# Gating two groups of tokens at a time in a gated-attention and top-2 expert kernel

## The chip, the cores and the metric

One core of a Trainium2 chip runs the whole kernel. The metric is the device time of one execution in microseconds (us). The engines meant below are TensorE (PE, its weight loads PEld), VectorE (DVE), ScalarE (ACT), GpSimd (POOL) and SyncE (SP). SP and POOL issue the transfers: SP the plain ones, POOL the indirect ones, whose rows go to or come from addresses that the kernel has computed. Each engine runs its own queue strictly in order, so an instruction that waits holds up everything behind it on that engine.

## The reference

The first half is a gated linear attention with a complex decay, the second a top-2 mixture of 8 experts on its output.

```python
# q, k, v, a_re, a_im: (4, 8, 768, 48), B=4 batches, H=8 heads
mag = np.sqrt(a_re * a_re + a_im * a_im)
scale = np.minimum(mag, 0.999) / (mag + 1e-06)
for t in range(S):
    S = (a * scale)[t] * S + k[t] v[t]^T          # complex state, 48 x 48 per head
    y[t] = q[t] @ S.real
x = y.transpose(0, 2, 1, 3).reshape(3072, 384)
noisy = x @ w_gate + log1p(exp(x @ w_noise)) * noise       # (3072, 8)
top2, weights = two largest of noisy, softmax over the two
out[t] = sum over the two experts e of weight * (relu(x[t] @ w1[e]) @ w2[e])   # 384 -> 1024 -> 384
```

(The recurrence and the last lines are abridged here.)

## The kernel before

**Attention.** The 3072 tokens are 24 tiles of 128: six groups g = 0 to 5 (blocks of the sequence), with B = 4 tiles in each (one per batch). Tile n is tile n % 4 of group n // 4. For each tile PE transposes q and k (`tr_unit`, L293), multiplies them (`sc_unit`, L302), DVE masks the product (L303), and `y_unit` (L349 and L351) multiplies by v and by the state, after which ACT copies the result out of PSUM into `xT` (L352, remembered as `YC[n]`). `x_unit` turns that tile into rows of tokens and ACT writes them into `xr` (L360), the buffer from which rows are sent on. A buffer `xr` holds the four tiles of one group, 400 numbers of each token.

**Gating.** When the tiles of a group are done, `gate_logits` (L363 to 376) multiplies them by the gate weights, turns the result and leaves 16 logits of each token in `lz`. `gate_dispatch` (L386 to 421) then runs a chain of some 28 short DVE instructions with three ACT exponentials among them (`gates` and `softplus`, L36 to 74): noisy logits, the two best experts of each token (L57 and L59, one instruction for each tile), their weights, which go straight into `xr` (L73). A few small matmuls (L397 and L399) count how many tokens each expert has received so far, from the one-hot rows `ohs` (L392), and the slots `sl` follow from the counts (L409). Groups 0 to 3 are gated whole. Groups 4 and 5 are gated as three tiles and then one.

**Scatter.** For each of its tiles and each of the two experts POOL issues one indirect transfer of 128 rows from `xr` to `xs`, a table in DRAM with 3072 rows for each expert (L413): 8 transfers for a group, 48 in all. In groups 0 to 3 those of tile b = 1, 2, 3 are made to wait for `YC` of one tile of the next group each:

```python
if g < NG - 2 and b:
    behind.append((d, B * (g + 1) + b - 1))
```

SP also writes the rows of the group to `xd` (L410), which only a fallback reads.

**Experts.** `load_x(0, 0, xga)` (L443) brings the first 512 rows of expert 0 from `xs` to SBUF. It reads the table that the scatters write, so it waits until every scatter that stands before it in the program, those of groups 0 to 4, has landed. `x_T(0, 0)` copies two columns of them (DVE, L497 and L498) and turns them on PE (L504), ACT and DVE split them into a high and a low part (L506 and L507), and `mm1` (L519) and `mm2` (L543) follow, expert after expert, until the end.

**Order.** The functions are put on a list of steps (`at(step, function)`), and the framework's scheduler, with a priority for gating (`hg`, `hl`) and for `x_unit` (`hx`), merges the steps into one queue for each engine. Queues are fixed before the run. ACT changes between two function tables, one for exponentials and one for sines, in numbered phases (`phase`), and the exponentials of group g's gating belong to phase 2 min(g + 3, 6).

Of the kernel before, what the change touches and what calls it, by code (L numbers as in the profile page):

```python
# [9 lines left out]
F32 = mybir.dt.float32  # L10
# [67 lines left out]
def kernel(  # L78
# [8 lines left out]
    nc = tc.nc  # L87
    NT, C, _, HD = qk.shape
    NG = NT // B
    S = NG * C  # L90
    D = HD // H
    N, DM = out.shape
# [102 lines left out]
    def phase(i, *args, **kw):  # L195

        if i not in phases:
            phases[i] = [nc.scalar.preload_act_table_set(("natural_log_exp_and_others", "trig_and_small")[i % 2])]
        phases[i].append(nc.scalar.activation(*args, **kw))  # L199
# [12 lines left out]
        nc.sync.dma_start(QK[n], qk[n])  # L212

    def load_v(n):
        V[n] = pa.tile([128, H, D], F32, name="v", bufs=6)
        nc.sync.dma_start(V[n].rearrange("p h d -> p (h d)"), v[n])

    def flat(t):
# [116 lines left out]
    def y_unit(n):  # L335

        b, g = bt(n)
        if b == 0:
            XR[g] = pa.tile([128, B, ROW], F32, name="xr", bufs=2)
            nc.gpsimd.memset(XR[g][:, :, RNO + 1:ROW], 0.0)  # L340
            nc.gpsimd.tensor_copy(XR[g][:, :, RNO], tokid[:, g])
        XT[n] = pa.tile([128, H // 2, 128], F32, name="xT", bufs=6)
        for i in range(H // 2):
            for z in range(0 if g else 1, 2):
                for r in range(2):
                    h = 2 * i + r
                    o = pY[64 * r:64 * r + D, i, :]
                    if z == 0:
                        nc.tensor.matmul(o, Z[b][:, h, :], QT[n][:, h, :], start=True, stop=False, skip_group_check=True)  # L349
                    else:  # L350
                        nc.tensor.matmul(o, V[n][:, h, :], AM[n][:, h, :], start=not g, stop=True, skip_group_check=True)  # L351
        YC[n] = nc.scalar.activation(XT[n], pY, AF.Copy)  # L352
# [7 lines left out]
        nc.scalar.copy(XR[g][:, b, 0:DM].rearrange("p (h d) -> p h d", h=H),  # L360
                       p.rearrange("p (h x) -> p h x", h=H)[:, :, 0:D])

    def gate_logits(g, lo, hi):  # L363
        n = hi - lo
        p = psC.tile([128, 512], F32, name="cum")
        for i in range(H // 2):
            for b in range(n):
                nc.tensor.matmul(p[32 * b:32 * b + 32, 0:128], wg[:, i, :], XT[B * g + lo + b][:, i, :],
                                 start=(i == 0), stop=(i == H // 2 - 1), tile_position=(0, 32 * b), skip_group_check=True)
        lt = pa.tile([128, 128], F32, name="lt")[0:32 * n]  # L370
        nc.scalar.copy(lt, p[0:32 * n, 0:128])
        p = psC.tile([128, 512], F32, name="cum")
        nc.tensor.transpose(p[:, 0:32 * n], lt, ident[0:32 * n, 0:32 * n])
        lz = pa.tile([128, B, 2 * E], F32, name="lz")[:, 0:n, :]
        nc.vector.tensor_copy(lz, p[:, :n * 32].rearrange("p (b x) -> p b x", b=n)[:, :, 0:2 * E])
        return lz

    def gate_tr(pool, ps, xt, b):
        p = ps.tile([128, 512], F32, name="cum")
# [3 lines left out]

    scat, behind, YC = [], [], {}

    def gate_dispatch(g, lo, hi, lz):  # L386
        n = hi - lo
        oh = gates(nc, pa, lz, nz[:, g, lo:hi], iota8, n, f"ga{n}",
                   lambda *a: phase(2 * min(g + 3, NG), *a),
                   XR[g][:, lo:hi, DM:DM + E])  # L390
        ohs = pa.tile([128, n, E], BF16, name=f"ohs{n}")
        nc.vector.tensor_add(ohs, oh[:, 0], oh[:, 1])  # L392
        p = psC.tile([128, 512], F32, name="cum")
# [13 lines left out]
        sl = pa.tile([128, 2, n], U32, name=f"sl{n}", bufs=2)  # L407
        with nc.allow_low_precision("whole numbers"):
            nc.vector.tensor_reduce(sl, oh, axis=AX.X, op=OP.add)  # L409
        nc.sync.dma_start(xd[(g * B + lo) * C:(g * B + hi) * C].rearrange("(b s) r -> s b r", b=n), XR[g][:, lo:hi, 0:DM + E])  # L410
        for b in range(n):
            for kk in range(2):
                d = nc.gpsimd.indirect_dma_start(  # L413
                    out=xs, out_offset=bass.IndirectOffsetOnAxis(ap=sl[:, kk, b:b + 1], axis=0),
                    in_=XR[g][:, lo + b, :], in_offset=None, bounds_check=E * N - 1, oob_is_err=False)
                for s in scat:
                    tc.declare_no_dep(d.ins, s.ins, reason="slots differ")
                scat.append(d)

                if g < NG - 2 and b:  # L420
                    behind.append((d, B * (g + 1) + b - 1))


    fill = {}
# [1 line left out]
    def at(step, f, *a):  # L426
        fill.setdefault(step, []).append((f, a))

    LZ = {}

    def glog(g, lo, hi):
        LZ[g, lo] = gate_logits(g, lo, hi)

    def gdis(g, lo, hi):
        gate_dispatch(g, lo, hi, LZ[g, lo])


    x3 = xs.rearrange("(e i) r -> e i r", e=E)
# [96 lines left out]
    def mm2(e, w):  # L535
        for j in ((0, 1, 2, 3), (4, 5, 6) if e + 1 < E else (6, 4, 5))[w]:
# [8 lines left out]
            else:  # L545
# [13 lines left out]
                in_=a, in_offset=None, bounds_check=N - 1, oob_is_err=False)  # L559


    P = dict(la=10, p1=7, d1=1, p2=6, dt=0, ds=0, lqk=6, p3=4, d3=0, q=2, lv=5, xu=0.5, ss=3, gl=0, gd=0.25,
             tr=1.4, sc=-0.2, st=0.05, y=0.2, up=0.4, w1=18, w2=21, xt=23, m1=23.3, dm=0.2, co=6, hg=50,
             hx=50, hl=200, s0=(7, 5.5, 4.5), s1=(7.5, 6, 5), qd=0.05, tk=0.2, th=0.05, sh=0.05)
    pri = {gdis: P["hg"], x_unit: P["hx"], glog: P["hl"]}
# [17 lines left out]
    for n in range(NT):  # L583
# [8 lines left out]
        at(n + P["up"], st_upd, n)  # L592
        at(n + .5 + P["xu"], x_unit, n)
        at(n + .5 + P["ss"], st_scale, n)
    for g in range(NG):
        for lo, hi in ((0, B),) if g < NG - 2 else ((0, B - 1), (B - 1, B)):
            at(B * g + hi + .5 + P["gl"], glog, g, lo, hi)
            at(B * g + hi + .5 + P["gd"], gdis, g, lo, hi)
        if g == NG - 2:
            at(B * g + hi + .5 + P["gd"], load_x, 0, 0, xga)  # L600

# [273 lines left out]
```

## Time and profile before

| | |
|---|---|
| time, median of 3 runs | 739.68 us (739.3 to 739.75) |
| the profiled execution | 739.76 us, of which the span in the trace is 738.0 us |
| PE busy | 699.7 us, 95% |
| DVE, ACT, POOL busy | 411.3, 342.5 and 166.1 us |

The span is the time from the first to the last instruction; some 1.8 us lie around it. Attention takes about the first 260 us, the experts the rest. A PE that shows as busy may still issue its matmuls further apart than it could, since their ends are modelled. Idle time of an engine matters only where another waits for that engine.

### The profile page before, as it was taken

The page shows a single profiled execution, that of the slowest core. Times are in us where ns is not written, and L with a number is a line of the kernel's source. Part 1 is how long each engine was busy: PE and PEld are TensorE (multiplying, and loading weights), DVE is VectorE, ACT ScalarE, POOL GpSimd, SP SyncE. Part 2 cuts the span into 40 slices and gives each one's busy share as a digit, 9 for nine tenths or more (in the row PEclk, how much of TensorE's full clock was granted, in tenths as well). Part 3 has the DMA queues.
Part 4 walks back from the last instruction along what each step waited for, and adds up shares of the span by engine and source line. Part 5 has one row for each costly group of instructions (what it writes and reads, how often), then busy time and mean ns, then how long its engine had stood idle before and what let it go on. Part 6 is the DMA issues. An engine that isn't in the chain of part 4 may idle for free. (4 is left out here: it accounts for less than half of the span.)

```text
span 738.0 us, 13470 instructions
## 1 busy us (share of the span) xinstructions
PE 699.7 (95%) x5184; PEld 622.5 (84%) x5184; DVE 411.3 (56%) x929; ACT 342.5 (46%) x609; POOL 166.1 (23%) x187
## 2 busy tenths in 40 slices
PE   0798989999999999999999999999999999999996
PEld 0377878878888879979988998998997998998995
DVE  5598888989899472553353344435525525435311
ACT  6899989798966430443133233223304403413300
POOL 2000005050506341032213123124024024122212
PEclk9899999999999999999999999999999999999999
DMA  7467876462457541271253244226226135031101
GB/s 284 118 222 189 263 218 239 132 219 46 155 143 238 201 165 74 81 239 51 97 172 106 87 139 147 75 98 202 75 88 208 43 115 191 28 108 54 51 33 34
DMA packets 64090, 100.18 MB, mean 136 GB/s; under 512 B 26490, under 2 KB 46129, under 8 KB 64016
## 3 DMA queue, kind: packets, MB, share of 16 engines
q1 hardware_dynamic: 54464, 71.68, 31.2%
q0 software_dynamic: 9552, 27.54, 10.7%
q8 instruction: 43, 0.70, 0.4%
q14 instruction: 31, 0.25, 0.1%
HBM read 68.55 MB, written 32.08 MB: 136 GB/s over the span
## 5 line engine op out<-in xcount | busy, mean ns | idle before, releaser
L543 PE MATMUL po<-w2h,h 128*128 128x384 f32 x768 | 201.8, 339 | 0.0
L519 PE MATMUL ph<-x,w1h 128*128 128x320 f32 (+1 forms) x720 | 192.4, 351 | 0.3 <-ACT x L506 0.3
L543 PEld LDWEIGHTS po<-w2h,h 128*128 128x128 f32 x768 | 139.9, 188 | 0.1
L519 PEld LDWEIGHTS ph<-x,w1h 128*128 128x128 f32 x720 | 126.7, 188 | 15.6 <-ACT x L506 0.5
L543 PE MATMUL po<-w2l,h 128*128 128x384 f32 x384 | 129.7, 338 | 0.0
L524 DVE SCALAR_TENSOR_TENSOR h<-ph,h 128x256 fp32r<-128x256 f32 (+2 forms) x184 | 74.2, 433 | 99.4 <-ACT h L521 99.4
L557 POOL DMA_INDIRECT out_dram<-ao,ox x56 | 55.7, 994 | 319.8 <-DVE ao L556 276.3
L519 PE MATMUL ph<-x,w1l 128*128 128x320 f32 (+1 forms) x360 | 125.5, 349 | 0.0
L521 ACT ACTIVATE h<-ph 128x320 fp32r<-128x320 f32 (+1 forms) x120 | 61.5, 512 | 119.0 <-PE ph L519 113.6
L556 DVE SCALAR_TENSOR_TENSOR ao<-po,gw,ao 128x384 f32<-128x384 f32 (+1 forms) x56 | 34.5, 616 | 134.0 <-PE po L543 133.0
L413 POOL DMA_INDIRECT xs<-xr,sl x48 | 53.7, 1118 | 200.6 <-DMA xd<-xr 108.6
L506 ACT CAST x<-px 128x320 fp32r<-128x320 f32 (+1 forms) x45 | 21.8, 502 | 126.8 <-PE px L504 125.9
L519 PEld LDWEIGHTS ph<-x,w1l 128*128 128x128 f32 x360 | 67.6, 188 | 7.3
L543 PEld LDWEIGHTS po<-w2l,h 128*128 128x128 f32 x384 | 72.1, 188 | 0.0
L530 POOL DMA_INDIRECT ao<-out_dram,ox x49 | 49.0, 1000 | 36.8 <-DMA out_dram<-ao,ox 24.0
L302 PE MATMUL psc<-qT,kT 112*128 112x128 f32 x384 | 53.3, 277 | 0.0
L472 ACT CAST w2h<-raw 128x768 fp32r<-128x768 f32 x32 | 25.3, 833 | 52.9 <-PE po L548 49.3
L302 PEld LDWEIGHTS psc<-qT,kT 112*128 112x128 f32 x384 | 47.7, 191 | 2.5 <-issue 1.3
L351 PE MATMUL pY<-am,v 128*48 128x128 f32 x384 | 42.6, 275 | 4.1 <-DVE am L303 4.1
L303 DVE TENSOR_TENSOR am<-psc,mask 128x512 f32<-128x512 f32 x48 | 32.6, 687 | 16.2 <-PE psc L302 16.1
L349 PE MATMUL pY<-qT,z 112*48 112x128 f32 x320 | 37.4, 276 | 0.0
L250 PE MATMUL cum<-t,tri_t 128*128 128x384 f32 x48 | 20.0, 545 | 17.6 <-ACT t L199 17.1
(206 smaller groups left out, 1019.6 us busy)
## 6 DMA issues: line engine op xcount, KB each, us to landing
raw<-in_moe_w_dram SPq DMA_DIRECT2D x24, 512.0 KB
raw<-in_moe_w_dram SPq DMA_DIRECT2D x32, 384.0 KB
qk<-in_qk_dram SPq DMA_DIRECT2D x24, 384.0 KB
xga<-xs SPq DMA_DIRECT2D x8, 800.0 KB
re<-in_a_dram SPq DMA_DIRECT2D x12, 384.0 KB
im<-in_a_dram SPq DMA_DIRECT2D x12, 384.0 KB
v<-in_v_dram SPq DMA_DIRECT2D x24, 192.0 KB
out_dram<-zero SPq DMA_DIRECT2D x12, 384.0 KB
```

Of the source, the lines that this page charges most:

```text
L302: nc.tensor.matmul(p[:, j, :], KT[n][:, h, :], QT[n][:, h, :], start=True, stop=True)
L303: nc.vector.tensor_mul(AM[n][:, 4 * half:4 * half + 4, :], p, mask[:, None, :].to_broadcast([128, 4, 128]))
L349: nc.tensor.matmul(o, Z[b][:, h, :], QT[n][:, h, :], start=True, stop=False, skip_group_check=True)
L351: nc.tensor.matmul(o, V[n][:, h, :], AM[n][:, h, :], start=not g, stop=True, skip_group_check=True)
L413: d = nc.gpsimd.indirect_dma_start(out=xs, out_offset=bass.IndirectOffsetOnAxis(ap=sl[:, kk, b:b + 1], axis=0), in_=XR[g][:, lo + b, :], i ...
L519: nc.tensor.matmul(p[:, :n], W1[kk][i][:, f * 128:(f + 1) * 128], XW[w, kk][:, j, :], start=(m == 0), stop=(m == len(ms) - 1))
L521: nc.scalar.activation(h[:, 0:n], p[:, :n], AF.Relu)
L524: nc.vector.scalar_tensor_tensor(h[:, dst:dst + b - a], p[:, a:b], 0.0, h[:, a:b].bitcast(F32), op0=OP.max, op1=OP.subtract)
L530: nc.gpsimd.indirect_dma_start(out=ao[j][0:w, :], out_offset=None, in_=out, in_offset=bass.IndirectOffsetOnAxis(ap=OX[e][0:w, j:j + 1], ax ...
L543: nc.tensor.matmul(p[:, :DM], HT[w, f][i][:, o:o + 128], W2[f // 2][k2][:, f % 2, :], start=(m == 0), stop=(m == len(ms) - 1))
L556: nc.vector.scalar_tensor_tensor(a, p[0:n, :DM], g, a, op0=OP.mult, op1=OP.add)
L557: nc.gpsimd.indirect_dma_start(out=out, out_offset=bass.IndirectOffsetOnAxis(ap=OX[e][0:n, j:j + 1], axis=0), in_=a, in_offset=None, bound ...
```

## The change

The gating of groups 0 and 1 is done in one pass, and so is that of groups 2 and 3. Groups 4 and 5 are gated as before, as three tiles and one. `gate_logits` is still run for each group, into its half of a shared `lz`. The exponentials of the pairs fall into phases 8 and 12. The weights of a pass now go into a tile `gw`, and POOL copies them from there into `xr` (L391 of the changed kernel), for each group. The write to `xd` thus waits for POOL and no longer for DVE. The 16 scatters of a pair stand one behind another, those of tile b = 1 to 7 behind the `YC` of tile 4 (g + 1) + b - 1, where g is the later group of the pair. So for groups 2 and 3 tile b = 5, 6, 7 (in group 3) waits for `YC[20]`, `YC[21]`, `YC[22]`.

`xr` gets 4 buffers in place of 2, `v` gets 5 in place of 6 and is loaded one step later, and the table in SBUF that the indirect transfers use takes 4 KB of each partition in place of 16 KB.

```diff
-        V[n] = pa.tile([128, H, D], F32, name="v", bufs=6)
+        V[n] = pa.tile([128, H, D], F32, name="v", bufs=5)
...
-            XR[g] = pa.tile([128, B, ROW], F32, name="xr", bufs=2)
+            XR[g] = pa.tile([128, B, ROW], F32, name="xr", bufs=4)
...
-    def gate_dispatch(g, lo, hi, lz):
-        n = hi - lo
-        oh = gates(nc, pa, lz, nz[:, g, lo:hi], iota8, n, f"ga{n}",
-                   lambda *a: phase(2 * min(g + 3, NG), *a),
-                   XR[g][:, lo:hi, DM:DM + E])
+    def gate_dispatch(gs, lo, hi, lz):
+        k = hi - lo
+        n, g = k * len(gs), gs[-1]
+        gw = pa.tile([128, n, E], F32, name=f"gw{n}")
+        oh = gates(nc, pa, lz, nz[:, gs[0]:g + 1, lo:hi].rearrange("p g b e -> p (g b) e") if k == B else nz[:, g, lo:hi],
+                   iota8, n, f"ga{n}", lambda *a: phase(2 * min(g + 3, NG), *a), gw)
+        for i, x in enumerate(gs):
+            nc.gpsimd.tensor_copy(XR[x][:, lo:hi, DM:DM + E], gw[:, i * k:(i + 1) * k])
...
-        nc.sync.dma_start(xd[(g * B + lo) * C:(g * B + hi) * C].rearrange("(b s) r -> s b r", b=n), XR[g][:, lo:hi, 0:DM + E])
+        for x in gs:
+            nc.sync.dma_start(xd[(x * B + lo) * C:(x * B + hi) * C].rearrange("(b s) r -> s b r", b=k), XR[x][:, lo:hi, 0:DM + E])
...
-                    in_=XR[g][:, lo + b, :], in_offset=None, bounds_check=E * N - 1, oob_is_err=False)
+                    in_=XR[gs[b // k]][:, lo + b % k, :], in_offset=None, bounds_check=E * N - 1, oob_is_err=False)
...
-                if g < NG - 2 and b:
-                    behind.append((d, B * (g + 1) + b - 1))
+                if len(gs) > 1 and b:
+                    behind.append((d, B * (g + 1) + (b - 1) // (1 if g < B else 2)))
...
-    P = dict(la=10, p1=7, d1=1, p2=6, dt=0, ds=0, lqk=6, p3=4, d3=0, q=2, lv=5, xu=0.5, ss=3, gl=0, gd=0.25,
+    P = dict(la=10, p1=7, d1=1, p2=6, dt=0, ds=0, lqk=6, p3=4, d3=0, q=2, lv=4, xu=0.5, ss=3, gl=0, gd=0.25,
...
-    for g in range(NG):
-        for lo, hi in ((0, B),) if g < NG - 2 else ((0, B - 1), (B - 1, B)):
-            at(B * g + hi + .5 + P["gl"], glog, g, lo, hi)
-            at(B * g + hi + .5 + P["gd"], gdis, g, lo, hi)
+    for gs in ((0, 1), (2, 3), (4,), (5,)):
+        for lo, hi in ((0, B),) if len(gs) > 1 else ((0, B - 1), (B - 1, B)):
+            for g in gs:
+                at(B * g + hi + .5 + P["gl"], glog, gs, g, lo, hi)
+            at(B * g + hi + .5 + P["gd"], gdis, gs, lo, hi)
...
-    nc = _bacc.Bacc("TRN2", target_bir_lowering=False, num_devices=1)
+    nc = _bacc.Bacc("TRN2", target_bir_lowering=False, num_devices=1, dynamic_dma_scratch_size=4096)
```

The changed lines move work in the queues. Lines of the changed kernel are 2 to 8 higher: L415 are its scatters, L398 and L400 its counting matmuls, L503 its copy of `gw` from `xga`, L510 its transposes of `xga`, L525 its `mm1`.

POOL's queue before, from the scatters of group 2 to those of group 5. The buffers `xr_1427`, `xr_1992`, `xr_2545` and `xr_3128` are those of groups 2, 3, 4 and 5:

```order
L413 DMA xs<-xr_1427,sl4_2148 24576x400 x8
L340 MEMSET xr_2545 128x4x7
L341 COPY xr_2545<-tokid_89 128x4
L413 DMA xs<-xr_1992,sl4_2705 24576x400 x8
L340 MEMSET xr_3128 128x4x7
L341 COPY xr_3128<-tokid_89 128x4
L413 DMA xs<-xr_2545,sl3_3075 24576x400 x6
L413 DMA xs<-xr_2545,sl1_3214 24576x400 x2
L413 DMA xs<-xr_3128,sl3_3502 24576x400 x6
L413 DMA xs<-xr_3128,sl1_3642 24576x400 x2
```

The same stretch of the changed kernel, where the buffers of groups 2, 3, 4 and 5 are `xr_1343`, `xr_1973`, `xr_2444` and `xr_3096`:

```order
L391 COPY xr_1343<-gw8_2548 128x4x8
L391 COPY xr_1973<-gw8_2548 128x4x8
L415 DMA xs<-xr_1343,sl8_2644 24576x400 x8
L415 DMA xs<-xr_1973,sl8_2644 24576x400 x2
L391 COPY xr_2444<-gw3_2992 128x3x8
L415 DMA xs<-xr_1973,sl8_2644 24576x400 x2
L415 DMA xs<-xr_2444,sl3_3043 24576x400 x6
L415 DMA xs<-xr_1973,sl8_2644 24576x400 x2
L391 COPY xr_2444<-gw1_3144 128x8
L415 DMA xs<-xr_2444,sl1_3184 24576x400 x2
L415 DMA xs<-xr_1973,sl8_2644 24576x400 x2
L391 COPY xr_3096<-gw3_3424 128x3x8
```

The last six scatters of group 3, two each behind `YC[20]`, `YC[21]` and `YC[22]`, now stand among the eight of group 4; before, all of group 3 stood ahead of group 4.

PE's queue before, at the end of `y_unit` of the last tile, 23, and the first transposes of `xga`:

```order
L349 MATMUL pY<-qT,z_794 48x128 x2
L351 MATMUL pY<-am,v 48x128 x2
L504 MATMUL ptr<-ident,xga 128x128 x7
L399 LDWEIGHTS tri_b
L399 MATMUL cum<-ohs_3486,tri_b 128x8
L359 MATMUL cum<-ident,xT 128x128 x4
L397 LDWEIGHTS ones_b
L397 MATMUL cum<-ohs_3486,ones_b 128x8
```

The same in the changed kernel, from the last counting matmul of group 5's first three tiles to the first matmuls of the experts:

```order
L398 LDWEIGHTS ones_b
L398 MATMUL cum<-ohs_3458,ones_b 128x8
L368 MATMUL cum<-xT,wg 32x128 x4
L510 MATMUL ptr<-ident,xga 128x128 x4
L373 MATMUL cum<-ident,lt 128x32
L510 MATMUL ptr<-ident,xga 128x128 x4
L525 MATMUL psc<-x_3400,w1h_2855 128x512 x2
L510 MATMUL ptr<-ident,xga 128x128 x4
L525 MATMUL psc<-x_3400,w1h_2855 128x512
L525 MATMUL psc<-x_3400,w1l_2856 128x512
```

The transposes of `xga` moved behind the counting, `x_unit` and logits of the last tiles; behind them only the expert's matmuls and one transpose of logits (L373) are left.

DVE's queue before, at its copy out of `xga`:

```order
L303 TENSOR_TENSOR am_3318<-psc_3332,mask_61 128x512
L303 TENSOR_TENSOR am_3369<-psc_3370,mask_61 128x512
L497 COPY gw_3426<-xga_94 128x4
L498 CAST ox_3427<-xga_94 128x4
L375 COPY lz_3424<-cum_3422 128x48
```

And in the changed kernel:

```order
L404 TENSOR_TENSOR base_run_87<-base_run_87,cum_3460 128x8
L407 TENSOR_TENSOR ga3oh_3445<-ga3oh_3445,pos3_3470 128x48
L410 TENSOR_REDUCE sl3_3474<-ga3oh_3445 128x6
L503 COPY gw_3396<-xga_94 128x4
L504 CAST ox_3397<-xga_94 128x4
L374 COPY lz1_3553<-cum_3561 128x16
```

The copy moved from ahead of the gating of group 5's first three tiles to behind it.

Counted over the whole program, DVE has 970 instructions in place of 1008, ACT 6 fewer, POOL 8 copies more, and PE 32 small matmuls more (L398 and L400), with their weight loads.

## Rows read from the trace of the kernel before

**Rows 1.** The page: its span, and the granted clock of TensorE in 40 slices, in tenths of full speed.

```profile
span 738.0 us, 13470 instructions
...
PEclk9899999999999999999999999999999999999999
```

**Rows 2.** The busy time of each engine in three stretches: attention at its steady pace, the seam between attention and experts, the experts. Columns: stretch, its length with PE's busy time and instructions, PEld, DVE, ACT, POOL, the granted clock, the share of the DMA engines, GB/s.

```profile
40.00:240.00 200.00, 193.48 (x2279) 163.07 (x2278) 176.18 (x402) 171.13 (x308) 42.02 (x42) 1.00 0.60 188
240.00:262.00 22.00, 20.50 (x233) 17.37 (x232) 11.48 (x64) 9.84 (x23) 6.17 (x7) 1.00 0.50 178
262.00:738.00 476.00, 468.30 (x2590) 431.25 (x2590) 201.27 (x420) 132.65 (x234) 112.64 (x114) 1.00 0.33 106
```

**Rows 3.** What PE waited for from 40 to 240 us: the waiting line, the one waited for, us in total, times, longest.

```profile
PE pY L351 <- DVE am L303: 3.1, 4, 1.3
PE cum L399 <- DVE ohs L392: 1.4, 2, 1.3
PE pG L312 <- DVE z L324: 1.1, 2, 0.7
PE cum L250 <- DVE t L245: 0.5, 1, 0.5
PE ptr L293 <- ACT kT L294: 0.2, 1, 0.2
```

**Rows 4.** DVE in the gating of a group: its instructions on 64, 32 and 32 numbers of each partition, by shape (busy us, mean ns of one).

```profile
L61 DVE TENSOR_TENSOR ga4oh<-iota,ga4ix 128x64 f32<-128x64 f32 x1 | 0.2, 218 | 0.0
...
L53 DVE TENSOR_TENSOR ga4c<-ga4c,lz 128x32 f32<-128x32 f32 x1 | 0.2, 186 | 0.0
```

**Rows 5.** DVE's timeline in the gating of group 0 (start, length): one of its instructions and the one behind it. The distance of their starts is what the instruction costs the queue.

```profile
105.37 0.19 DVE L53 TENSOR_TENSOR ga4c<-ga4c,lz 128x32 f32<-128x32 f32 x1
105.47 0.95 DVE L231 CUSTOM_DVE_ANT_0 t<-t 128x768 f32<-128x768 f32 x1
```

**Rows 6.** PE's timeline at the counting matmuls of group 0, and at those of group 1, of which 13 start from 146.05 until 146.45: start, length, line, count, and in brackets the idle time before.

```profile
109.48 0.17 PE L399 MATMUL cum<-ohs,tri_b 128*128 128x8 bf16 x1 [1.27 <-DVE ohs L392]
...
146.05 0.17 PE L397 MATMUL cum<-ohs,ones_b 128*128 128x8 bf16 x1
...
146.45 0.65 PE L312 MATMUL pG<-v,kh 128*48 128x48 f32 x10
```

**Rows 7.** POOL's timeline: a copy of token numbers into `xr`, the first and the last of the eight scatters of group 3, the first and the last of the eight of group 4.

```profile
199.71 0.67 POOL L341 COPY xr<-tokid 128x4 f32<-128x4 f32 x1
220.96 1.67 POOL L413 DMA_INDIRECT xs<-xr,sl  x1 [20.58 <-ACT xT L352]
...
231.14 1.64 POOL L413 DMA_INDIRECT xs<-xr,sl  x1 [0.30 <-issue]
...
237.89 0.99 POOL L413 DMA_INDIRECT xs<-xr,sl  x1 [2.53 <-DVE sl L409]
...
247.03 0.97 POOL L413 DMA_INDIRECT xs<-xr,sl  x1 [0.31 <-issue]
```

**Rows 8.** ACT's timeline: `YC[20]` and `YC[22]`.

```profile
237.76 0.60 ACT L352 ACTIVATE xT<-pY 128x512 f32<-128x512 f32 x1 [0.85 <-PE pY L351]
...
250.56 0.60 ACT L352 ACTIVATE xT<-pY 128x512 f32<-128x512 f32 x1 [1.31 <-PE pY L351]
```

**Rows 9.** SP's timeline: the issue of the first load of `xga`.

```profile
250.45 0.33 SPq L443 DMA_DIRECT2D xga<-xs  x1
```

**Rows 10.** DVE's timeline: its copy that waits for that load.

```profile
254.71 0.17 DVE L497 COPY gw<-xga 128x4 f32<-128x4 f32 x1 [2.38 <-DMA xga<-xs]
```

**Rows 11.** The scatters issued from 235 to 250 us: from issue to landing.

```profile
DMA to landing us min/median/max: 3.3/5.2/7.0
```

**Rows 12.** The same for those issued from 260 to 275 us.

```profile
DMA to landing us min/median/max: 2.6/2.6/4.0
```

**Rows 13.** PE's timeline at the seam: the last tile's `y_unit`, the first 7 of 12 transposes of `xga`, two of the experts' matmuls ahead, the logits of the last tile, the last four transposes, and the experts' matmuls steadily from 261.83.

```profile
256.39 0.43 PE L351 MATMUL pY<-am,v 128*48 128x128 f32 x4 [0.96 <-DVE am L303]
...
257.19 0.98 PE L504 MATMUL ptr<-ident,xga 128*128 128x128 f32 x7
...
259.44 0.71 PE L519 MATMUL psc<-x,w1h 128*128 128x512 f32 x2
260.08 1.06 PE L368 MATMUL cum<-xT,wg 128*32 128x128 f32 x8
261.07 0.66 PE L504 MATMUL ptr<-ident,xga 128*128 128x128 f32 x4
...
261.83 0.50 PE L519 MATMUL psc<-x,w1h 128*128 128x512 f32 x1
262.17 0.39 PE L519 MATMUL psc<-x,w1l 128*128 128x512 f32 x1
262.40 0.64 PE L519 MATMUL psc<-x,w1h 128*128 128x512 f32 x2
```

**Rows 14.** Busy time and granted clock in three stretches near the start (columns as in rows 2).

```profile
21.70:28.60 6.90, 2.47 (x6) 0.61 (x5) 1.11 (x2) 6.87 (x10) 0.00 (x0) 1.00 0.63 181
28.60:35.40 6.80, 5.92 (x31) 3.96 (x32) 5.94 (x7) 6.77 (x16) 0.00 (x0) 0.50 0.58 133
35.40:42.00 6.60, 6.35 (x70) 5.69 (x67) 5.94 (x10) 4.92 (x10) 0.00 (x0) 1.00 0.79 198
```

**Rows 15.** What SP's queue waited for longest from 40 to 240 us.

```profile
SPq L216 <- PE pY L351: 37.0, 11, 10.3
```

More of the change, by code (lines that the diff above doesn't have):

```diff
@@ L361, in x_unit, with gate_logits @@
                        p.rearrange("p (h x) -> p h x", h=H)[:, :, 0:D])
-    def gate_logits(g, lo, hi):
+    def gate_logits(g, lo, hi, lz):
         n = hi - lo
@@ L373, in gate_logits @@
         nc.tensor.transpose(p[:, 0:32 * n], lt, ident[0:32 * n, 0:32 * n])
-        lz = pa.tile([128, B, 2 * E], F32, name="lz")[:, 0:n, :]
         nc.vector.tensor_copy(lz, p[:, :n * 32].rearrange("p (b x) -> p b x", b=n)[:, :, 0:2 * E])
-        return lz
     def gate_tr(pool, ps, xt, b):
@@ L429, with glog, gdis @@
     LZ = {}
[L431 to L435, printed above, removed]
+    def glog(gs, g, lo, hi):
+        k = hi - lo
+        if g == gs[0]:
+            LZ[gs, lo] = pa.tile([128, k * len(gs), 2 * E], F32, name=f"lz{k * len(gs)}", bufs=2 if len(gs) > 1 else 1)
+        i = gs.index(g)
+        gate_logits(g, lo, hi, LZ[gs, lo][:, i * k:(i + 1) * k])
+    def gdis(gs, lo, hi):
+        gate_dispatch(gs, lo, hi, LZ[gs, lo])
     x3 = xs.rearrange("(e i) r -> e i r", e=E)
```

## The prediction

> **What bounds the kernel now.** I read the 40 slices first, then three stretches by engine, then what PE waited for, and last the timelines of POOL, SP, DVE and PE at the seam between attention and experts. The span is 738.0 us at a TensorE clock near full nearly throughout [rows 1]. PE is busy for 193.48 of 200 us in steady attention and for 468.30 of 476 us in the experts [rows 2], so PE is the bound in both. DVE (176.18) and ACT (171.13) are close behind it in attention. PE's idle time there is 200 - 193.48 = 6.5 us, and the waits name 6.3 of it, 6.1 for DVE [rows 3]. Work taken from DVE can win at most about that; a wait of PE at the seam is lost in full, for the experts behind it have no slack.
>
> At the seam, POOL's last scatter of group 4 starts at 247.03 [rows 7], SP issues the load of `xga` at 250.45 [rows 9], DVE reads it at 254.71 [rows 10], and PE turns it at 257.19 [rows 13]. The load is 2.5 us early for PE.
>
> **The change part by part.** The sum is made against the profiled execution, 739.76 us (738.0 of span and 1.8 around it); the median is 0.08 lower.
>
> *Counting on PE.* A pass over n tiles takes n(n-1)/2 + 2n small matmuls: 14 for four, 44 for eight. Two passes of 44 replace four of 14, 32 more. In group 1, 13 of them take 146.45 - 146.05 = 0.40 us, 0.031 each [rows 6]. 32 x 0.031 = **+1.0 us** on the engine that is the bound.
>
> *Short instructions on DVE.* There are 38 fewer. One costs its queue 105.47 - 105.37 = 0.10 us [rows 5], so 3.8 us go. Those left work on twice as many numbers: 32 more cost 218 - 186 = 0.032 us [rows 4], and a pass has ten on 64 in place of 32 and four on 128 in place of 64: 10 x 0.032 + 4 x 0.064 = 0.58, for two passes 1.2. DVE saves 2.6 us of 176. Little of it lies on the path directly; what counts is PE's waits for DVE. The longest, 1.27 us in the gating of group 0 [rows 6], has no successor, since group 0 is no longer gated by itself. Bounds: all 6.3 us of waits go [rows 3], or each of the two passes meets a wait of 1.3 where 1.4 stand now, +1.2. I take the 1.3 and a further 0.7 for DVE's lighter queue, **-2.0 us**, nearer to the single row than to the whole list.
>
> *The seam.* Now `load_x` waits for group 3's scatters behind `YC[20]` to `YC[22]`, and POOL has, in this order, two behind `YC[20]`, six of group 4, two behind `YC[21]`, a copy, two of group 4, two behind `YC[22]`. `YC[20]` ends at 237.76 + 0.60 = 238.4 [rows 8]; the ten scatters of the pair ahead fit in before, as the eight of group 3 took from 220.96 to 231.14 [rows 7]. So POOL starts the 14 at about 238.5. Scatters without a wait start (247.03 - 237.89) / 7 = 1.306 us apart [rows 7]: the last starts 13 x 1.306 = 17.0 later, plus 0.7 for the copy, of which the nearest row is 0.67 [rows 7]: 256.2. `YC[22]` ends at 251.2 [rows 8], so POOL's own queue is later than the wait. From the last scatter's start to SP's issue it takes 250.45 - 247.03 = 3.42, from there to DVE's read 254.71 - 250.45 = 4.26 [rows 7, 9, 10]. `xga` is there at 256.2 + 3.42 + 4.26 = 263.9.
>
> PE reaches it sooner. DVE's copy of `gw` no longer stands ahead of the last gating, so its wait of 2.38 us there [rows 10] and PE's 0.96 for the mask behind it [rows 13] go, and `y_unit` is done near 256.2. From 257.19 to 261.07 lie counting, `x_unit` and logits with 8 transposes (0.9) and two expert matmuls (0.5) among them, 3.9 - 1.4 = 2.5 us without these [rows 13]: PE is at the transposes by about 259 and idles from 259 to 263.9. Behind it come 12 transposes (some 0.11 each, 1.3) and a turn of logits (0.2), and 0.8 of waiting for ACT and DVE to split, as between 257.19 and 261.83 now, 4.6 us with some 3.8 of work in them [rows 13]. The experts' matmuls run as if begun at 263.9 + 2.3 = 266.2. Before, they run steadily from 261.83 with two done ahead, worth 2 x (262.40 - 262.17) = 0.46 [rows 13]: as if from 261.4. **+4.8 us**, with nothing behind to make it up. Ends: landing in 2.6 as the latest scatters do [rows 12], and a copy of 0.1, give 3.4; landing in 7.0 [rows 11] gives 8.4.
>
> The scatters' pace is a choice. In group 3 they stood (231.14 - 220.96) / 7 = 1.454 us apart, in a stretch where DVE was busier [rows 7]; by that the last starts 1.9 us later. The Trainium skill, page "SBUF — State Buffer", section on the two separate sides, says that DVE, in an operation that takes both ports, keeps GpSimd from writing the descriptors of its transfers. By that rule it would be 1.454 wherever DVE is dense, and the sum 1.9 higher. I keep 1.306, the row of the same place, where DVE is busy for 11.48 of 22 us [rows 2].
>
> *At nothing.* The other copies on POOL: the scatters of group 3 find it idle for 20.58 us now [rows 7], and without that cover they would cost some 0.7 each. SP's wait for `xd`, now for POOL: loads queue behind it, but SP waits 37.0 us for free `v` buffers [rows 15], and PE waits for no load [rows 3]; without that slack each wait would hold up q and k by its length. Five `v` buffers and the later load: same reason. Six ACT instructions fewer: no wait for ACT to speak of [rows 3]. Four `xr` buffers: no row of a wait for them. The small table of the indirect transfers: nothing in the trace shows one, so a rival.
>
> Sum: 739.76 + 1.0 - 2.0 + 4.8 = 743.56, less 0.08: **743.5 us**.
>
> **The rivals.** (1) *Attention gains more than the seam loses.* If DVE is what sets PE's pace, all 6.3 us of waits go. For it: DVE is 88% busy; PE's named waits are nearly all for DVE. Against: 2.6 us are little of 176, and the two passes are longer chains. With the seam at its low end: 739.7 + 1.0 - 6.3 + 3.4 = 737.8, faster. It decides when attention wins over 3.4 + 1.0 + 1.5 = 5.9 us. (2) *They cancel.* Attention wins 4 us and the seam loses 3.4: 739.7 + 1.0 - 4.0 + 3.4 = 740.1. (3) *The clock falls.* After 6.9 us with 2.47 of matmul time the granted clock was 0.50, 1.2 GHz, for the next 6.8 us [rows 14]. If PE's idle 5 us does this once, matmuls for 6.8 us take twice as long, +3.4: 746.9. Against: no stretch after 42 us has done it, but none has such a gap. The Trainium skill, page "TensorE: Matmul & The Clock Gate", section "Why this matters for your kernels", advises against idle gaps between bursts because the array goes back to the slow clock; by that rule this rival is the forecast. (4) *The small table stops POOL*, so that a scatter starts only when the one before has landed, 2.6 us apart [rows 12] in place of 1.306: 13 x 1.3 = 17 more, 760. No wait of this kind is in the trace.
>
> **How the numbers follow.** Forecast 0.53, its own range 741.2 to 746.5; rival 1 0.14; rival 2 0.20; rival 3 0.10; rival 4 0.03. A measurement tells some 0.2%, 1.5 us, from no change: 738.2 to 741.2. Slower: 0.53 + 0.10 + 0.03 = 0.66. Same 0.20, faster 0.14. The range leaves out rival 4, most of rival 1 and the top of rival 3: 738.6 to 747.0.
>
> **What would show it.** In the changed profile: PE idle for some 5 us in front of L510, ended by the transfer into `xga`; POOL's 14 scatters from `YC[20]` on with no gap over 0.4 us; the load issued near 260. L400 waits at two places only, and DVE busy some 3 us less. `YC[20]` about 1 us earlier. I am wrong if the load lands before PE gets to L510, if POOL starts the six of group 4 with waits between, if `YC[20]` moves by more than 3 us either way, or if the experts' stretch changes its length.

## The result, and the profile after

The changed kernel takes 744.31 us, median of 4 runs (744.06 to 744.5), beside 739.49 (738.53 to 739.75) of the kernel before: 1.0068 of it, 95% interval 1.0053 to 1.0083. The profiled execution has a span of 742.6 us in place of 738.0. (The runs half_pace, late_pace, store_only and no_xd5 below were made where the kernels took 13 to 26 us longer than in the other runs, the one before 765.0, with DVE held up for as much as 12 us while POOL's scatters ran; they are compared with that 765.0 alone.)

The three stretches after, columns as in [rows 2]:

```profile
40.00:240.00 200.00, 196.10 (x2308) 163.01 (x2307) 173.23 (x362) 169.93 (x301) 36.71 (x37) 1.00 0.58 178
240.00:262.00 22.00, 17.35 (x217) 15.47 (x214) 10.81 (x61) 8.67 (x20) 13.04 (x15) 1.00 0.72 250
262.00:738.00 476.00, 471.87 (x2605) 434.06 (x2605) 203.27 (x424) 133.99 (x236) 113.88 (x115) 1.00 0.33 107
```

In attention DVE is busy for 2.95 us less and PE idles for 3.9 us in place of 6.5 [rows 2]; but `YC[20]` stands at 237.78, where it stood [rows 8]. At the seam PE is busy for 3.2 us less and POOL for 6.9 more. PE's waits over the whole run, without the longest, which is near the start and stood there before (16.5 us, before 17.1; columns as in [rows 3]):

```profile
PE ptr L510 <- DMA xga<-xs: 4.8, 1, 4.8
...
PE pY L351 <- DVE am L303: 1.6, 3, 0.9
PE cum L270 <- DVE tf L255: 1.4, 2, 1.0
PE cum L400 <- DVE ohs L393: 1.4, 2, 1.3
```

The first is new. POOL's timeline shows where it comes from: the pair's 16 scatters begin at 222.28, when the slots of groups 2 and 3 are there; ten are started, POOL waits 0.89 us for `YC[20]`, and group 4's eight and the other six of group 3 follow without a gap.

```profile
222.28 1.24 POOL L415 DMA_INDIRECT xs<-xr,sl  x1 [2.90 <-DVE sl L410]
...
236.50 0.98 POOL L415 DMA_INDIRECT xs<-xr,sl  x1 [0.30 <-issue]
237.47 0.27 POOL L391 COPY xr<-gw 128x24 f32<-128x24 f32 x1
238.63 0.99 POOL L415 DMA_INDIRECT xs<-xr,sl  x1 [0.89 <-ACT xT L352]
...
255.47 0.98 POOL L415 DMA_INDIRECT xs<-xr,sl  x1 [0.30 <-issue]
```

Before, the last one ahead of the load started at 247.03 [rows 7], and group 2's eight had gone out from 186.71 on:

```profile
186.71 0.99 POOL L413 DMA_INDIRECT xs<-xr,sl  x1 [23.92 <-DVE am L303]
...
196.81 0.97 POOL L413 DMA_INDIRECT xs<-xr,sl  x1 [0.30 <-DMA xs<-xr,sl]
```

In the changed kernel SP issues the load at 258.16 (250.45 before [rows 9]), and right behind it the write of 588 KB of group 5 to `xd`, which stood at 260.33 before, behind the landed load. DVE sees `xga` at 263.72 (254.71 before [rows 10]). SP, whose second line takes that write and the next one together, then DVE:

```profile
258.16 0.33 SPq L449 DMA_DIRECT2D xga<-xs  x1
258.59 14.04 SPq L412 DMA_DIRECT2D xd<-xr  x2
```

```profile
263.72 0.17 DVE L503 COPY gw<-xga 128x4 f32<-128x4 f32 x1 [5.32 <-DMA xga<-xs]
```

PE does nearly all that the last group leaves to it, counting and logits, while the load is under way, then idles for 4.76 us. The experts' matmuls run steadily from 267.34, where they did from 261.83 [rows 13]:

```profile
256.78 0.18 PE L400 MATMUL cum<-ohs,tri_b 128*128 128x8 bf16 x1 [1.26 <-DVE ohs L393]
...
258.01 1.06 PE L368 MATMUL cum<-xT,wg 128*32 128x128 f32 x8 [0.39 <-ACT xr L360]
263.83 1.09 PE L510 MATMUL ptr<-ident,xga 128*128 128x128 f32 x4 [4.76 <-DMA xga<-xs]
...
267.34 0.47 PE L525 MATMUL psc<-x,w1h 128*128 128x512 f32 x1
```

Four transposes take 1.09 us, where four took 0.66 before [rows 13]: the granted clock is 0.50 (1.2 of 2.4 GHz) behind the gap. Columns as in [rows 2]:

```profile
259.80:263.80 4.00, 0.00 (x0) 0.00 (x0) 0.08 (x1) 0.00 (x0) 0.00 (x0) 0.99 0.91 278
263.80:266.60 2.80, 2.77 (x11) 2.30 (x12) 1.20 (x5) 1.15 (x3) 1.81 (x2) 0.50 0.39 147
```

### The profile page after: what moved, and what is told of

Read it like the earlier page. It is cut to its first block, busy times and chain, and to the rows that moved or that the text cites. A ratio compares the mean times of both kernels' runs of the same rounds, so it can differ in the third digit from the quotient of the medians.

```text
span 742.6 us, 13465 instructions
## 1 busy us (share of the span) xinstructions
PE 703.4 (95%) x5216; PEld 623.9 (84%) x5216; DVE 410.3 (55%) x891; ACT 342.0 (46%) x603; POOL 170.8 (23%) x195
## 4 chain that ended last, share of the span: by engine, by line
PE 87%; DVE 4%; DMA 4%; ACT 3%; issue 1%; POOL 1%; SPq 0%; POOLq 0%; DVEq 0%; ACTq 0%
PE ph L525 28%; PE po L549 27%; PE ptr L293 5%; PE psc L302 4%; PE pG L312 3%; PE px L510 3%; PE cum L250 2%; PE psc L525 2%; PE cum L270 2%; PE pY L351 2%; PE pY L349 2%; PE po L554 2%; PE po L557 2%; PE cum L359 1%; DMA raw<-in_moe_w_dram 1%; ACT t L199 1%
## 5 line engine op out<-in xcount | busy, mean ns | idle before, releaser
L525 PE MATMUL ph<-x,w1h 128*128 128x320 f32 (+1 forms) x720 | 192.4, 351 | 0.3 <-ACT x L512 0.3
L525 PEld LDWEIGHTS ph<-x,w1h 128*128 128x128 f32 x720 | 126.7, 188 | 15.7 <-ACT x L512 0.5
L525 PE MATMUL ph<-x,w1l 128*128 128x320 f32 (+1 forms) x360 | 125.4, 349 | 0.0
L525 PEld LDWEIGHTS ph<-x,w1l 128*128 128x128 f32 x360 | 67.6, 188 | 7.3
L415 POOL DMA_INDIRECT xs<-xr,sl x48 | 54.3, 1131 | 37.2 <-ACT xT L352 11.7
L391 POOL COPY xr<-gw 128x32 f32<-128x32 f32 (+2 forms) x8 | 2.6, 334 | 171.0 <-DVE gw L73 171.0
```

The costliest lines, as they stand in the source:

```text
L415: d = nc.gpsimd.indirect_dma_start(out=xs, out_offset=bass.IndirectOffsetOnAxis(ap=sl[:, kk, b:b + 1], axis=0), in_=XR[gs[b // k]][:, lo + ...
L525: nc.tensor.matmul(p[:, :n], W1[kk][i][:, f * 128:(f + 1) * 128], XW[w, kk][:, j, :], start=(m == 0), stop=(m == len(ms) - 1))
```

## The experiments

My first theory was: the loss is the seam, and it comes from the place of group 3's last scatters, which wait for `YC[19]` to `YC[22]` and so stand among group 4's. Rivals: pairing costs in itself; the storage costs.

**half_pace and half_pace_2: the pair paced sooner.**

```diff
-                    behind.append((d, B * (g + 1) + (b - 1) // (1 if g < B else 2)))
+                    behind.append((d, B * (g + 1) + (b - 1) // (1 if g < 2 else 2)))
```

> The changed kernel with one number other: the scatters of group 3 (tiles b = 4 to 7 of the second pair) stand behind YC[17] to YC[19] in place of YC[19] to YC[22]; all else stays. Theory (the loss is the seam, made by group 3's scatters that stand among those of group 4 on POOL): the load of xga goes out near 250.5 again, PE idles under 1 us in front of L510, the granted clock stays near 1, and the time falls by 4 to 6 us, to 738.3 to 740.3. Rival (pairing itself costs: longer DVE chains, 32 more counting matmuls, the small table): the time stays above 742.

> The kernel of half_pace once more (scatters of group 3's tiles behind YC[17] to YC[19] in place of YC[19] to YC[22], all else as changed), for a run in which the kernel before takes some 739.5 us as it did beside the changed kernel, and not 765. Theory (the loss is the seam, made by group 3's scatters that stand among those of group 4): load of xga issued near 250.5, PE idle under 1 us in front of L510, 738.3 to 740.3 us. Rival (pairing itself costs the 4.8 us): above 742. If the kernel before takes some 765 us again, so that DVE stands still during POOL's scatters: this kernel has 3 to 8 us less than it, since it has fewer such stretches.

half_pace took 763.03 us beside 765.0, 0.998 [0.9955, 1.0005], and tells little. half_pace_2 took **748.63** beside 739.45, 1.0122 [1.0104, 1.0140]: slower than the change itself. The theory missed. The rival's bound, above 742, holds, but the 4.8 us that it ascribed to pairing don't explain 4.3 more. POOL first:

```profile
222.00 1.23 POOL L415 DMA_INDIRECT xs<-xr,sl  x1 [2.91 <-DVE sl L410]
...
244.06 0.97 POOL L415 DMA_INDIRECT xs<-xr,sl  x1 [0.30 <-issue]
245.02 0.23 POOL L391 COPY xr<-gw 128x24 f32<-128x24 f32 x1
...
254.67 0.98 POOL L415 DMA_INDIRECT xs<-xr,sl  x1 [0.30 <-issue]
```

With the waits gone, 24 scatters run back to back and the last starts 0.80 us sooner. So the pacing isn't the cause, **POOL's own time is**: 16 + 8 scatters, 1.42 us apart in the mean (32.67 us from the first to the last), behind 222 us, where before 8 + 8 stood behind 220.96, since group 2's eight had gone out earlier. I could have read that from the first and last scatter of the pair. The rest of the loss shows in DVE's queue, and in PE's behind it (half_late, below, tells the two apart):

```profile
262.98 0.17 DVE L503 COPY gw<-xga 128x4 f32<-128x4 f32 x1 [11.00 <-DMA xga<-xs]
```

```profile
264.66 0.67 PE L351 MATMUL pY<-am,v 128*48 128x128 f32 x4 [9.58 <-DVE am L303]
...
266.12 1.76 PE L510 MATMUL ptr<-ident,xga 128*128 128x128 f32 x7
...
270.07 1.06 PE L368 MATMUL cum<-xT,wg 128*32 128x128 f32 x8
```

The order fixed ahead of the run counted on an early load and put DVE's copy from `xga` ahead of the last tile's mask, as in the kernel before. PE's counting and logits, which the changed kernel does while it waits, come behind the load here.

**late_pace and store_only: the kernel before with one part of the change.** late_pace moves group 3's scatters behind `YC[20]` to `YC[22]`, store_only takes the storage alone.

```diff
-                    behind.append((d, B * (g + 1) + b - 1))
+                    behind.append((d, B * (g + 1) + b - 1 + (B if g == 3 else 0)))
```

```diff
-        V[n] = pa.tile([128, H, D], F32, name="v", bufs=6)
+        V[n] = pa.tile([128, H, D], F32, name="v", bufs=5)
-            XR[g] = pa.tile([128, B, ROW], F32, name="xr", bufs=2)
+            XR[g] = pa.tile([128, B, ROW], F32, name="xr", bufs=4)
-    nc = _bacc.Bacc("TRN2", target_bir_lowering=False, num_devices=1)
+    nc = _bacc.Bacc("TRN2", target_bir_lowering=False, num_devices=1, dynamic_dma_scratch_size=4096)
```

(and `lv=5` to `lv=4`)

> The kernel before with one thing other: the scatters of group 3's tiles b = 1, 2, 3 stand behind YC[20], YC[21], YC[22] in place of YC[16] to YC[18]. No pairing, 16 KB table, 6 v buffers. Theory (the place of these scatters is the loss): on POOL 14 scatters again stand between YC[20] and the load, two of them behind YC[22], which ends near 251.2; the load goes out at 256 to 258, PE waits 2 to 5 us for it, and the time is 742 to 745. Rival (pairing itself costs): 739 to 740, as before.

> The kernel before with the changed storage alone: table of the indirect transfers 4 KB, xr in 4 buffers, v in 5 buffers and loaded one step later. No pairing, pacing as before. Theory (these cost nothing): 738.5 to 740.5, scatters on POOL still about 1.3 us apart where nothing holds them. Rival (the small table or the fewer v buffers cost part of the 4.8 us): above 741, with scatters further apart or PE waiting for v.

late_pace: 761.66 beside 765.0, 0.9963 [0.9943, 0.9983]. store_only: 766.21 beside 765.0, 1.0031 [1.0008, 1.0053]. Both missed the times expected, which were meant beside some 739.5. DVE's stops, 13.1 us in late_pace's profile, are larger than any loss that it was to show, so it decides nothing. The storage costs at most a half per cent there; pair01, below, has it nearly whole and shows no loss.

**pair01 and pair23: each half of the change.**

```diff
-    for gs in ((0, 1), (2, 3), (4,), (5,)):
+    for gs in ((0, 1), (2,), (3,), (4,), (5,)):
```

and for pair23 `((0,), (1,), (2, 3), (4,), (5,))`. In both, `xr` has 3 buffers in place of 4, and a group that is gated by itself keeps the pacing of the kernel before (those lines are left out here).

> Half of the change: groups 0 and 1 gated together, groups 2 and 3 each by itself with the pacing of the kernel before; 3 xr buffers, all else as changed (weights through gw and POOL, 4 KB table, 5 v buffers). New theory, after half_pace_2 in which POOL's 24 scatters ran from 222.00 to 254.67 without a wait and the load still came late: the loss is POOL's time, since the pair (2, 3) has its slots only at 222 and its 16 scatters stand ahead of group 4's 8. So without that pair group 2's scatters lie in POOL's idle time before 200 again, the last one ahead of the load starts near 247, PE does not idle in front of L510, and the time is 738.5 to 740.5. Rival (pairing in itself costs, in DVE's chain and PE's counting): half of the loss stays, 741.5 to 742.5.

> The other half of the change: groups 0 and 1 each gated by itself, groups 2 and 3 together, paced as in the changed kernel; 3 xr buffers, all else as changed. New theory (24 scatters on POOL from about 222 on): last one ahead of the load at 254 to 256, load of xga issued near 258, PE idle for 4 to 5 us in front of L510, 743.0 to 745.0. Rival (pairing in itself costs): 741.5 to 742.5.

pair01 took **739.12** beside 738.82, 1.0006 [0.9993, 1.0019]; pair23 **747.11**, 1.0107 [1.009, 1.0125]. The first pair costs nothing that can be told from noise, the second by itself as much as the whole change and more. In pair01 the last scatter ahead of the load starts at 248.22. In pair23 it starts at 259.94, later than in the change, and the time lies outside the 743.0 to 745.0 expected: POOL's fill of the next `xr` stands between the pair's scatters and waits for one of three buffers, which is my edit's doing.

```profile
234.04 1.54 POOL L415 DMA_INDIRECT xs<-xr,sl  x1 [0.30 <-issue]
239.52 0.12 POOL L340 MEMSET xr<- 128x28 f32 x1 [3.94 <-DMA xs<-xr,sl]
```

```profile
268.32 1.09 PE L510 MATMUL ptr<-ident,xga 128*128 128x128 f32 x4 [8.77 <-DMA xga<-xs]
```

So the last scatter 4.5 us later (259.94 for 255.47) gave PE 4.0 us more of waiting (8.77 for 4.76) and a time 2.8 us longer: the seam follows POOL.

**wide_count: fewer counting matmuls.**

```diff
+        nc.tensor.matmul(p[:, 0:n * E], tri_b, ohs.rearrange("p n e -> p (n e)"), start=True, stop=False, skip_group_check=True)
+        for j in range(1, n + 1):
+            nc.tensor.matmul(p[:, j * E:(n + 1) * E], ones_b, ohs[:, 0:n + 1 - j, :].rearrange("p n e -> p (n e)"),
+                             start=False, stop=(j == n), skip_group_check=True)
```

> The changed kernel with the counting matmuls made wide: one over all columns of ohs with tri_b, then for j = 1 to n one with ones_b that adds all tiles j places on; 9 in place of 44 in a pass over eight tiles, 4 in place of 9 over three. 80 fewer in all, the sums are the same. By the price of the prediction (0.031 each) and as both passes stand on PE ahead of POOL's scatters: 70 x 0.031 = 2.2 less, 741.8 to 742.6. Rival (PE's counting lies beside other work and costs nothing): 744.0 to 744.6.

**743.59** beside 738.82, 1.0058 [1.0042, 1.0073]: by the ratios 0.7 us less than the change, where 1.7 to 2.5 were expected; by the medians as much above its kernel before as the change (4.77 for 4.82). The intervals overlap. On PE the second pass, first of the change and then of wide_count, takes 218.74 - 217.03 = 1.71 and 217.95 - 217.10 = 0.85 us:

```profile
217.03 0.17 PE L400 MATMUL cum<-ohs,tri_b 128*128 128x8 bf16 x1 [0.16 <-DVE ohs L393]
...
218.40 0.34 PE L398 MATMUL cum<-ohs,ones_b 128*128 128x8 bf16 x8
```

```profile
217.10 0.19 PE L395 MATMUL cum<-ohs,tri_b 128*128 128x64 bf16 x1 [0.16 <-DVE ohs L393]
217.60 0.35 PE L397 MATMUL cum<-ohs,ones_b 128*128 128x64 bf16 x8
```

The price stands on PE (43 matmuls in 1.2 us, 0.028 each). Some of it passes through POOL: the last scatter starts 0.46 sooner than in the change, and `xga` is there 0.53 sooner. How much reaches the end these runs don't settle.

**no_xd5 and no_xd5_2: no write behind the load.** The write of group 5's rows to `xd` is left out.

```diff
-        for x in gs:
+        for x in gs if g < NG - 1 else ():
             nc.sync.dma_start(xd[...
```

> The changed kernel without the write of group 5's rows to xd (left out, only the fallback reads them), so that nothing of SP stands behind the load of xga at the seam. Theory (the write of 588 KB that is issued 0.4 us behind the load makes it slow): from issue to DVE's read it takes 4.1 to 4.5 us in place of 5.6, PE's idle time in front of L510 falls to 3.3 to 3.9, the time to 742.4 to 743.6. Rival (the load is slow for another reason, as the scatters of POOL): the load stays above 5.2 us and the time at 744.0 to 744.6.

> The kernel of no_xd5 once more (the changed kernel without the write of group 5's rows to xd; that part of the work is left out), for a run in which the kernel before takes some 739 us. Theory (the write that is issued 0.4 us behind the load of xga slows it): load 4.2 to 4.5 us in place of 5.56, PE idle in front of L510 for 3.4 to 3.8, time 0.8 to 1.6 us under the changed kernel's 744.3: 742.7 to 743.5. Rival (the load is slow for another reason): load 5.4 to 5.7, 744.0 to 744.6.

no_xd5: 755.32 beside 765.0, 0.990 [0.9868, 0.9932]. no_xd5_2: **742.57** beside 738.68, 1.0049 [1.0034, 1.0064]: 1.4 us under the change by the ratios, and 3.89 us above its kernel before where the change is 4.82; the intervals overlap, so the gain in time isn't clear of noise. The load's gain is plain in the trace: it takes 261.76 - 257.43 = 4.33 us in place of 5.56 (SP, DVE):

```profile
257.43 19.19 SPq L449 DMA_DIRECT2D xga<-xs  x2
```

```profile
261.76 0.17 DVE L503 COPY gw<-xga 128x4 f32<-128x4 f32 x1 [4.20 <-DMA xga<-xs]
```

In half_pace_2 too, where that write came late, it took 262.98 - 258.65 = 4.33; in pair23, with the write 0.43 us behind, 268.20 - 262.62 = 5.58. In no_xd5_2 PE waits 3.63 us in place of 4.76.

**warm_gap: PE kept busy in the gap.**

```diff
+            if e == 0 and w == 0 and kk == 0:
+                for _ in range(42):
+                    WARM.append(nc.tensor.transpose(p[:, 0:128], ident, ident))
```

(put behind the logits of the last tile by a dependence that only sets the order)

> The changed kernel with 42 more transposes of ident on PE, into a tile that is overwritten at once, put behind the logits of the last tile and ahead of the transposes of xga, so that PE is busy for some 4.6 us of the 4.8 that it idled. Part of PE's, ACT's and DVE's order behind them moves (the last gating stands a little sooner). Theory (the granted clock fell to 0.50 from 263.7 to 267.1 because PE had been idle, and that cost about 1 us): the clock stays at 1.00, four transposes of xga take 0.4 to 0.5 us in place of 1.1, and the time is 743.0 to 743.8. Rival (the clock falls for another reason, or its cost is hidden behind ACT's and DVE's splitting): 744.0 to 744.8.

**748.73** beside 738.68, 1.0137 [1.0115, 1.0158]: a miss by 5 us, though the clock did as expected. Eight transposes take 1.06 us, and the clock is 1.00 (PE, then the windows):

```profile
262.52 1.06 PE L513 MATMUL ptr<-ident,xga 128*128 128x128 f32 x8
```

```profile
260.00:264.00 4.00, 3.58 (x33) 3.36 (x32) 1.08 (x8) 0.42 (x2) 0.84 (x1) 1.00 0.76 260
264.00:268.00 4.00, 1.81 (x10) 1.26 (x10) 3.51 (x20) 1.38 (x4) 3.07 (x4) 1.00 0.43 157
```

The gain is lost in the order that moved with it: the last gating now stands ahead of the experts (they run steadily from 267.50, 267.34 in the change), and later DVE's copy from `xgb` stands ahead of work that PE needs. DVE, PE:

```profile
281.73 0.17 DVE L503 COPY gw<-xgb 128x3 f32<-128x3 f32 x1 [3.82 <-DMA xgb<-xs]
```

```profile
282.83 1.22 PE L528 MATMUL psc<-x,w1h 128*128 128x512 f32 x2 [2.91 <-DVE h L533]
```

From 267.50 to the end it takes 3.8 us more than the change does from 267.34, and 2.9 of these are this wait; behind it the granted clock is 0.50 from 282.8 to 285.8. So the run shows that the gap is what lowers the clock, and not what that costs the whole.

**half_late: half_pace_2 with DVE's copy behind the mask.**

```diff
+    for c in CP[:2]:
+        tc.add_manual_dep(c.ins, MK[NT - 1].ins.name, after, reason="mask")
```

(`CP` holds DVE's copies from `xga`, `MK` the masks by tile.)

> The kernel of half_pace_2 with DVE's copy of gw from xga (L503) put behind the mask of the last tile (L303). In half_pace_2 it stood ahead of it, DVE waited 11.0 us for the load and PE 9.6 for the mask. POOL's 24 scatters run as there, so xga is there at 263 to 264. Theory (half_pace_2 was slower than the changed kernel by that place in DVE's queue, not by POOL): the mask is done near 252, y_unit by 256, PE waits at L510 for 6 to 8 us with counting, x_unit and logits of the last tiles still behind it; 745.3 to 746.7, 2 to 3 less than half_pace_2. Rival (DVE's wait is hidden behind PE's wait for xga): 748 to 749.

**748.37** beside 738.68, 1.0126 [1.0109, 1.0144]: no less than half_pace_2, the rival was right. The mask no longer waits, but PE's transposes of `xga` still stand ahead of the last group's work, and the copy still stands ahead of its gating:

```profile
263.52 1.73 PE L510 MATMUL ptr<-ident,xga 128*128 128x128 f32 x7 [7.00 <-DMA xga<-xs]
...
268.14 1.92 PE L368 MATMUL cum<-xT,wg 128*32 128x128 f32 x8
...
270.90 0.50 PE L525 MATMUL psc<-x,w1h 128*128 128x512 f32 x1
```

With `xga` there at 263.4 the experts run from 270.90; in the change, with 263.7, from 267.34. What stands behind the waiting transposes is worth 3.6 us, part of it at the low clock (the logits take 1.92 us, 1.06 at full speed).

**best1: the first pair, wide counting, the copy behind the mask.** The edits of pair01, wide_count and half_late in one, with single groups' weights straight into `xr`:

```diff
-        gw = pa.tile([128, n, E], F32, name=f"gw{n}")
+        gw = pa.tile([128, n, E], F32, name=f"gw{n}") if len(gs) > 1 else XR[g][:, lo:hi, DM:DM + E]
```

> Groups 0 and 1 together, the others as in the kernel before (weights of single groups straight into xr), wide counting (47 fewer matmuls than the kernel before), and DVE's copy of gw from xga put behind the mask of the last tile, so that DVE does not wait 2.4 us for the load ahead of it. 4 KB table, 3 xr and 5 v buffers. Theory: 739.5 less 47 x 0.031 = 1.5 less PE's 0.96 for that mask: 736.5 to 738.0, if the load comes no later than before. Rival (the load is then what PE waits for, and the gain is lost in front of L508): 738.5 to 739.5.

**738.89** beside 738.82, 1.0002 [0.9993, 1.0011]: no gain. The last scatter starts at 249.81 and `xga` is there at 256.82, 2.1 us later than before, so the rival's limit is nearer, though PE does not idle at the transposes. Where the 2.5 us expected went isn't settled: `YC[19]` stands 184.3 us behind `YC[0]` in place of 182.4, in the same way as in pair01, with no wait of PE named there. The loss lies between `YC[14]` and `YC[17]`, where group 2's scatters run: 32.2 us (32.1 in pair01) for 29.5 before. In the change, where group 2's scatters do not run there, it is 28.6.

The seam in one table: start of the last scatter ahead of the load, DVE's first read of `xga`, PE's wait that hangs on it, the ratio to the kernel before.

| kernel | last scatter | `xga` read | PE waits | ratio |
|---|---|---|---|---|
| before | 247.03 | 254.71 | 0.96 (mask) | 1 |
| pair01 | 248.22 | 257.21 | 2.55 (mask) | 1.0006 |
| best1 | 249.81 | 256.82 | none | 1.0002 |
| no_xd5_2 | 254.76 | 261.76 | 3.63 | 1.0049 |
| wide_count | 255.01 | 263.19 | 4.74 | 1.0058 |
| the change | 255.47 | 263.72 | 4.76 | 1.0068 |
| pair23 | 259.94 | 268.20 | 8.77 | 1.0107 |
| half_pace_2 | 254.67 | 262.98 | 9.58 (mask) | 1.0122 |
| half_late | 255.03 | 263.40 | 7.00 | 1.0126 |

In the four from no_xd5_2 to pair23 PE has the last group's counting and logits ahead of the transposes, and the ratio follows the last scatter. In half_pace_2 and half_late they stand behind, and the ratios are 1.0122 and 1.0126 with a last scatter near that of the change.

pair01's profiled execution was the longest of its twelve (741.88), with a load of 6.3 us that nothing in its trace explains; its median is 2.8 us shorter, so its row here is not that of a usual run.

## Why the prediction was right, step by step

The time is 0.8 us over the forecast of 743.5, and the loss is where it was put. That the sum comes so near is in part luck: attention came out 1.5 us worse than forecast and the seam 0.7, while 0.9 and 0.5 us that no term had (below) made up for most of it.

*Counting, +1.0.* The price holds on PE (0.028 for 0.031). How much of it shows in the time stays open: by wide_count's ratio some 0.01 for each of its 80 matmuls, which would make the term 0.3, by its median nothing, and its interval leaves room for most of the price.

*PE's waits, -2.0.* The waits went as forecast, PE idles 2.6 us less up to 240. The time did not follow: what PE no longer idled it was busy instead. From `YC[0]` to `YC[20]` it takes 237.78 - 46.38 = 191.4 us, before 237.76 - 46.88 = 190.9. So the net of this term and the counting was +0.5 where -1.0 stood, the mis-sized step of the sum. Some 0.9 us of the 2.6 are those matmuls (32 x 0.028); the rest I can't place. The first pair does no harm that pair01's interval shows, and no good.

*The seam, +4.8.* Measured 267.34 - 0.46 = 266.9 for 261.4, +5.5. Its steps: POOL's last scatter 255.47 for 256.2; from there to SP's issue 2.69 for 3.42; the load 5.56 for 4.26, as the write to `xd` now stands right behind it, which I named nowhere and no_xd5_2 shows (1.2 us of load; on the time 0.9 to 1.4, not clear of noise); `xga` there at 263.7 for 263.9, since these three cancel, which is luck too. From there to the experts 3.2 for 2.3, with the low clock.

*The pacing* stood in the working as the gate from which the 14 scatters start (238.5; measured 238.63). That was right as a time and misleading as a cause: POOL waited there for 0.89 us, and half_pace_2 shows nearly the same end of POOL's queue without it (254.67 for 255.47). The cause is that group 2's eight scatters moved from a stretch, from 186.71 on, behind which POOL still idled for 20.58 us [rows 7], into the row ahead of the load; in pair01 they go out from 188.14 again, and the loss is gone from the time.

*At nothing.* The small table: scatters that nothing holds are 1.28 us apart, as they were before (the 1.306 has slower ones among it), so rival 4 fell. The POOL copies take 0.22 to 0.27, not 0.7. No load but that of `xga` is among PE's waits.

*Rival 3, the clock*, came true in a smaller form: 0.50 for some 3 us behind a gap of 4.76. The Trainium skill, page "TensorE: Matmul & The Clock Gate", section "Why this matters for your kernels", warns of such gaps; warm_gap agrees, with 1.00 where the gap was filled. *Rivals 1 and 2* fell with the waits that weren't worth their length.

*Left over:* from the experts' begin to the end it takes 0.9 us less than before (742.6 - 266.9 and 738.0 - 261.4), and this execution began some 0.5 us sooner. What made them stays open.

## What to carry to other kernels

Work that is put together to save instructions comes out later and in one lump: count what each queue behind it, here POOL's scatters, must then do before the next thing that somebody waits for. A wait that stands in front of the lump may be mere slack; compare the queue's own time, number times pace, with the wait before blaming it. And where the order is fixed ahead of the run, a late transfer costs by what stands behind its first reader on each engine, so read the new order whenever an arrival moves.

## What the runs showed of the hardware

- A load of 800 KB took 4.26 to 4.34 us with no other transfer of SP until it had landed (before, half_pace_2, half_late, best1, no_xd5_2) and 5.47 to 5.58 with a write of 588 KB issued 0.43 us behind it (the change, pair23, wide_count, warm_gap). pair01's 6.31, without that write, is the exception.
- Behind a gap of 4.76 us the granted clock was 0.50 for some 3 us, and so it was behind waits of 2.55 (pair01, 258.8 to 262.0), 2.91 (warm_gap) and 3.63 (no_xd5_2, 261.8 to 264.8); in half_late, behind 7.00, it was 0.50 from 264 to 268. With the gap filled it stayed at 1.00.
- In half_pace POOL's scatters ran on at 1.28 us apart, and DVE began a multiplication only when 12 us had gone by. PE too started only three or four matmuls at a time, some 1.4 us apart, with no engine named for the waits (POOL, DVE, PE). In half_pace_2, the same kernel, DVE's and POOL's work alternated, and scatters took up to 1.82 us.

```profile
228.10 0.97 POOL L415 DMA_INDIRECT xs<-xr,sl  x1 [0.30 <-issue]
...
238.30 0.99 POOL L415 DMA_INDIRECT xs<-xr,sl  x1 [0.30 <-issue]
```

```profile
239.96 0.96 DVE L282 TENSOR_TENSOR kh<-qk,tr 128x768 f32<-128x768 f32 x1 [11.98 <-remote]
```

```profile
231.36 0.32 PE L351 MATMUL pY<-am,v 128*48 128x128 f32 x2 [1.00 <-issue]
```

The Trainium skill, page "SBUF — State Buffer", section "SBUF: two separate sides", says that of DVE and GpSimd, in operations that take the ports they share, the one that starts first holds them for its whole instruction, while the other waits. Here DVE waited over nine scatters and the 0.30 us between them, and PE was slowed as well, so the traces do not show that these ports are the cause. Why the same kernel does one or the other stays open.
